# Fused attention and two feed-forward layers on one core: rounding queries and keys of all units on ScalarE

## The chip, the cores and the metric

The kernel runs on one core of a Trainium2 chip. The metric is the device time of one execution in microseconds, as the median over runs. A NeuronCore has TensorE (PE in the profile; its weight loads have a row of their own, PEld), VectorE (DVE), ScalarE (ACT), GpSimd (POOL) and SyncE (SP), which issues most DMAs. Each engine executes its own instructions in the order in which they were written to its queue.

## The reference

Three layers follow each other; the output of one is the input of the next.

```
scores = q k^T / sqrt(D), minus a bias from the cumulated max(s, 0); causal
attn   = softmax(scores);  x = attn v           # 4 batches x 8 heads, 576 positions, D = 64
h = x w_in;  x = (h * sigmoid(1.702 h)) w_out   # 2304 tokens, 512 -> 2048 -> 512
h = x w_in2; x = (s2 * max(h, 0)^2 + b2) w_out2
```

All tensors are fp32.

## The kernel before

TensorE multiplies in a rounded fp32 format (fp32r). To keep the precision, most operands are split in two: `hi` is the operand rounded to fp32r, `lo` the rest, and a product becomes a sum of two or three products. Rounding is a copy to an fp32r tile; the rest is a subtraction.

Attention is cut into eight **units**: for each of the 4 batches the first half of the query positions (320 rows, three chunks of 64, 128 and 128) and the second half (256 rows, two chunks of 128). A unit has 8 heads, so there are 64 head steps, numbered n = 0 to 63; the first-half units come first (n = 0 to 31), then the second-half ones (n = 32 to 63). While a unit's attention runs, TensorE works at the same time on the first feed-forward layer of the unit before it; `run` merges the two into one hand-made order for TensorE. The other engines' orders in this part are set by a scheduler that simulates the program's time line; in the first heads SP is written by hand too. After the last attention step come the rest of the first layer and the second layer, in an order written by hand for all engines.

One head goes through four places of the code:

- `prep` (L239 to L281) loads queries and keys of one head, in two copies on 128 partitions, as `raw`, and splits them. For n below 8 there is no split. From n = 8 on `hi` is `raw` rounded (L271, through `scaled`, L116 to L123, so it appears as L119 on ScalarE and L123 on VectorE); SP copies the queries' part of `hi` to `lo` (L272); VectorE subtracts for the queries' rest (L273) and GpSimd for the keys' (L274, `lo`). `hi` has 640 columns in the first half and 832 in the second. Each of `raw` and `hi` has two buffers, `lo` one. Of every second head it also rounds the values `v` (L279, L280).
- `qk` (L283 to L314) multiplies queries and keys chunk by chunk into PSUM (`ps`, two buffers); VectorE adds the mask and keeps the running extreme (L300; a chunk with 576 keys goes in two pieces of 288, so a second-half head has three pieces: 448, 288 and 288), ScalarE takes the exponential and its row sums (L306). After the last chunk VectorE makes the reciprocals of the sums (L310, L311), and the chunks of `x` are scaled by them: the last one on ScalarE (L119), the others on GpSimd (L121).
- `transposes` (L316 to L341) turns the probabilities of the head before by TensorE into `pst` (two buffers), in two groups in the first half and three in the second; ScalarE takes each group out rounded (`ph`, L338), VectorE the rest (L341).
- `pv` (L343 to L370) multiplies with the values, two heads back.

Beside these, `h_item` (L433 to L450) makes the hidden layer: `ph` by TensorE (L421), tanh on ScalarE (`th`, L442), a multiply on VectorE (L443), rounding on ScalarE (`g`, L447) and its rest on GpSimd (L448). `y_item` (L454 to L473) multiplies `g` with the second weights (L461).

The choice of the engine that rounds `hi` is one expression:

```
scaled(nc.scalar if n < 2 * H else nc.vector, hi[:, : u.n + J], raw[:, : u.n + J])
```

H is 8, so heads 8 to 15 are rounded on ScalarE and heads 16 to 63 on VectorE: 16 of them in the first half, 32 in the second.

Of the kernel before, what the change touches and what calls it, by code (L numbers as in the profile page):

```python
# [42 lines left out]
def f32(ap):  # L43
    return ap.bitcast(F32)
# [27 lines left out]
def fused_kernel(ctx: ExitStack, tc: tile.TileContext, qkT, vP, s, w1i, w1o, w2i, w2o, s2, b2, out):  # L72
    nc = tc.nc
    B, H, _, _ = qkT.shape
# [41 lines left out]
    def scaled(engine, out, in_, scale=1.0):  # L116

        if engine is nc.scalar:
            nc.scalar.activation(out, in_, AF.Copy, scale=scale)  # L119
        elif engine is nc.gpsimd:  # L120
            nc.gpsimd.tensor_scalar(out=out, in0=in_, scalar1=scale, scalar2=0.0, op0=ALU.mult, op1=ALU.add)  # L121
        else:
            nc.vector.tensor_scalar(out=out, in0=in_, scalar1=scale, scalar2=None, op0=ALU.mult)  # L123
# [50 lines left out]
    with ExitStack() as p1:  # L174
# [61 lines left out]
        def tile(shape, name, dtype=F32):  # L236
            return ap.tile([P, *shape], dtype, tag=name, name=name, bufs=size["bufs"][name])

        def prep(n):  # L239
            u, h = units[n // H], n % H  # L240
            J, nj = u.i1, len(u.keys)
            raw = tile([size["n"] + size["keys"]], "raw")

            r = u.b * H + h
            qc, kc = (slice(0, u.n), slice(u.n, u.n + J)) if u.half == 0 else (slice(J, J + u.n), slice(0, J))
            src = qkT[u.b, h, :, : u.n + J] if u.half == 0 else qkT[u.b, h, :, u.i0 :]
            heads[n] = t = {"x": {}, "qc": qc, "kc": kc}

            def beside(to):
                nc.sync.dma_start(to[D:R, kc], rows_d[0, r, :, :J])  # L250
                nc.sync.dma_start(to[D:R, qc], rows_d[1, r, :, u.i0 : u.i1])

            if n < H:
                nc.sync.dma_start(raw[:D, : u.n + J], src[:D])
                if n > 0:
                    beside(raw)
            else:
                nc.sync.dma_start(raw[:, : u.n + J], src)
            if h % 2 == 0:
                vraw = tile([size["blocks"], P], "vraw")  # L260
                nc.sync.dma_start(vraw[:, :nj, :], vP[u.b, h // 2, :, :nj, :])
                vs[n] = vs[n + 1] = vraw
            if n < H:
                t["parts"] = [(raw, R)]
                return


            hi = tile([size["n"] + size["keys"]], "hi", F32R)
            lo = tile([size["n"] + size["keys"]], "lo", F32R)
            beside(f32(lo))  # L270
            scaled(nc.scalar if n < 2 * H else nc.vector, hi[:, : u.n + J], raw[:, : u.n + J])  # L271
            nc.sync.dma_start(f32(lo[:D, qc]), f32(hi[:D, qc]))  # L272
            nc.vector.tensor_tensor(hi[D:, qc], raw[D:, qc], f32(hi[D:, qc]), ALU.subtract)  # L273
            nc.gpsimd.tensor_tensor(lo[:D, kc], raw[:D, kc], f32(hi[:D, kc]), ALU.subtract)  # L274
            t["parts"] = [(lo, R), (hi, P)]
            if h % 2 == 0:
                v = tile([size["blocks"], 4, D], "v", F32R)
                src = vraw[:, :nj].rearrange("p j (a d) -> p j a d", a=2)
                scaled(nc.gpsimd if n < 2 * H else nc.vector, v[:, :nj, 0:4:3, :], src)  # L279
                nc.gpsimd.tensor_tensor(v[:, :nj, 1:3, :], src, f32(v[:, :nj, 0:4:3, :]), ALU.subtract)  # L280
                vs[n] = vs[n + 1] = v  # L281
# [106 lines left out]
        def prep_to(n):  # L388
            while n_prep[0] <= min(n, limit - 1):
                prep(n_prep[0])  # L390
                n_prep[0] += 1
# [633 lines left out]
```

## Time and profile before

| | |
|---|---|
| median of 3 runs | 1046.09 us (1045.94 to 1046.18) |
| the profiled execution | 1047.54 us |
| its span, first to last instruction | 1045.7 us |
| mean granted clock of TensorE | 0.997 |
| busy: TensorE, its weight loads | 1006.4 us (96%), 926.0 us (89%) |
| busy: VectorE, ScalarE, GpSimd | 655.7 us (63%), 589.7 us (56%), 347.1 us (33%) |

The table gives the busy time of each engine over the whole span, which is an average over parts with different limits. "PE busy" counts matmuls that overlap each other. The attention steps of the first-half units run up to about 300 us, those of the second-half units from there to about 595 us; what follows has no attention.

### The profile page before, as it was taken

To read this page: it belongs to the slowest core of one execution; us is meant where nothing else is said; L and a number is where in the kernel's file an instruction comes from. 1 tells how busy PE (TensorE), PEld (TensorE's weight loads), DVE (VectorE), ACT (ScalarE), POOL (GpSimd) and SP (SyncE) were. 2 spreads that over 40 slices of the span, in tenths; PEclk is the share of its full clock that TensorE was granted. 3 is DMA by queue.
4 is the path that set the end of the run, shared out by engine and by line. 5 is a ranking of instruction groups with operands and counts; after the bars stand their busy time and mean duration, and the time that the engine had idled before them with its cause. 6 is when DMAs were issued, how large, how long until landed. Compare 5 with 4: busy or idle time off the path is not lost.

```text
span 1045.7 us, 17713 instructions
## 1 busy us (share of the span) xinstructions
PE 1006.4 (96%) x6312; PEld 926.0 (89%) x6312; DVE 655.7 (63%) x1426; ACT 589.7 (56%) x1316; POOL 347.1 (33%) x381
## 2 busy tenths in 40 slices
PE   5889999999999999999999999999999999999998
PEld 3458999999989999999999999999989989899897
DVE  4689877566558788788878556566575333632232
ACT  4889856556626656656656645566464343543342
POOL 1115535335325346345435322011033442311110
PEclk9998999999999999999999999999999999999999
DMA  5675422122032232232221067766126436352321
GB/s 177 192 246 190 125 85 78 47 84 57 9 122 68 76 91 76 76 95 72 84 92 56 21 247 225 257 217 228 51 91 234 149 132 229 123 201 96 126 71 61
DMA packets 52879, 129.58 MB, mean 124 GB/s; under 512 B 7068, under 2 KB 19480, under 8 KB 52792
## 3 DMA queue, kind: packets, MB, share of 16 engines
q1 hardware_dynamic: 52584, 128.32, 37.3%
q8 instruction: 50, 0.82, 0.3%
q14 instruction: 37, 0.30, 0.1%
q10 hardware_dynamic: 208, 0.13, 0.0%
HBM read 95.45 MB, written 28.90 MB: 119 GB/s over the span
## 4 chain that ended last, share of the span: by engine, by line
PE 77%; DVE 12%; ACT 5%; DMA 3%; issue 2%; SPq 1%; POOL 0%; ACTq 0%; DVEq 0%; POOLq 0%
PE py L756 18%; PE py L461 15%; PE ph L421 14%; PE sum_p L730 6%; PE ph L806 5%; PE ps L294 4%; PE pst L332 4%; DVE hi L123 3%; PE sum_r L730 3%; PE po L359 3%; PE py L697 2%; DMA pair<-w1i 2%; DVE x L300 2%; PE sum_q L730 2%; ACT x L306 1%
## 5 line engine op out<-in xcount | busy, mean ns | idle before, releaser
L421 PE MATMUL ph<-xT,wi 128*128 128x320 f32 (+1 forms) x1536 | 244.9, 304 | 6.3 <-DVE th L443 2.6
L756 PE MATMUL py<-wo,g 128*128 128x512 f32 x864 | 223.1, 394 | 0.6 <-DVE g L793 0.6
L421 PEld LDWEIGHTS ph<-xT,wi 128*128 128x128 f32 x1536 | 215.6, 191 | 8.5 <-DVE th L443 3.2
L461 PE MATMUL py<-g,wo 128*128 128x320 f32 (+1 forms) x1344 | 215.3, 304 | 0.0
L461 PEld LDWEIGHTS py<-g,wo 128*128 128x128 f32 x1344 | 188.0, 189 | 0.9
L756 PEld LDWEIGHTS py<-wo,g 128*128 128x128 f32 x864 | 160.6, 188 | 26.2 <-DVE g L793 0.9
L448 POOL TENSOR_TENSOR g<-th,g 128x320 fp32r<-128x320 f32 (+1 forms) x128 | 113.0, 885 | 133.5 <-ACT g L447 124.2
L306 ACT ACTIVATE x<-x,m 64x64 f32<-64x64 f32 (+2 forms) x160 | 89.4, 559 | 99.7 <-DVE m L300 98.1
L274 POOL TENSOR_TENSOR lo<-raw,hi 64x576 fp32r<-64x576 f32 (+1 forms) x56 | 67.8, 1211 | 122.7 <-issue 57.1
L300 DVE CUSTOM_DVE_ANT_0 x<-ps,mask 64x64 f32<-64x64 f32 (+2 forms) x160 | 68.0, 426 | 51.6 <-PE ps L294 49.7
L332 PE MATMUL pst<-ident,x 128*128 128x128 f32 (+2 forms) x480 | 86.2, 288 | 10.0 <-DVE ph L341 8.2
L793 POOL TENSOR_TENSOR g<-odd,g 128x768 fp32r<-128x768 f32 x16 | 30.5, 1904 | 183.3 <-ACT g L790 183.3
L121 POOL TENSOR_SCALAR x<-x,tot 64x64 f32<-64x64 f32 (+1 forms) x96 | 49.5, 523 | 93.5 <-DVE tot L311 47.6
L730 PE MATMUL sum_p<-xs,part 128*128 128x384 f32 x384 | 78.5, 339 | 1.4 <-ACT e L828 1.2
L338 ACT ACTIVATE ph<-pst 64x256 fp32r<-64x256 f32 (+2 forms) x144 | 67.1, 473 | 20.7 <-PE pst L332 19.3
L332 PEld LDWEIGHTS pst<-ident,x 128*128 128x128 f32 (+2 forms) x480 | 54.8, 136 | 25.1 <-DVE ph L341 13.2
L730 PEld LDWEIGHTS sum_p<-xs,part 128*128 128x128 f32 x384 | 69.2, 188 | 7.4 <-ACT e L828 1.7
L442 ACT ACTIVATE th<-ph 128x320 f32<-128x320 f32 (+1 forms) x128 | 51.6, 403 | 42.2 <-PE ph L421 40.4
L443 DVE SCALAR_TENSOR_TENSOR th<-th,ph 128x320 f32<-128x320 f32 (+1 forms) x128 | 57.5, 449 | 27.5 <-ACT th L442 26.5
L447 ACT ACTIVATE g<-th 128x320 fp32r<-128x320 f32 (+1 forms) x128 | 56.4, 440 | 32.2 <-DVE th L443 31.7
L806 PE MATMUL ph<-xs,wi 128*128 128x384 f32 x384 | 71.8, 335 | 0.0
L828 ACT ACTIVATE e<-sum_p 128x384 f32<-128x384 f32 x48 | 23.5, 489 | 84.9 <-PE sum_p L730 84.9
(108 smaller groups left out, 1666.3 us busy)
## 6 DMA issues: line engine op xcount, KB each, us to landing
part<-parts_d SPq DMA_DIRECT2D x32, 512.0 KB
raw<-qkT SPq DMA_DIRECT2D x32, 416.0 KB
pair<-w1o SPq DMA_DIRECT2D x16, 512.0 KB
pair<-w1i SPq DMA_DIRECT2D x16, 512.0 KB
pair<-w2i SPq DMA_DIRECT2D x16, 512.0 KB
pair<-w2o SPq DMA_DIRECT2D x16, 512.0 KB
parts_d<-part SPq DMA_DIRECT2D x16, 512.0 KB
raw<-qkT SPq DMA_DIRECT2D x24, 320.0 KB
```

Source lines behind the costliest of these rows:

```text
L274: nc.gpsimd.tensor_tensor(lo[:D, kc], raw[:D, kc], f32(hi[:D, kc]), ALU.subtract)
L300: nc.vector.tensor_tensor_reduce(out=x[:w, j0:j1], in0=ps[:w, : j1 - j0], in1=mask[:w, WIDE - a0 + j0 : WIDE - a0 + j1], scale=-1.0 / ROOT ...
L306: nc.scalar.activation(x[:w, :a1], x[:w, :a1], AF.Exp, bias=least, scale=-1.0, accum_out=tot[:w, c : c + 1])
L332: nc.tensor.transpose(ps[: j1 - j0, at : at + a1 - a0], t["x"][c][: a1 - a0, j0:j1], ident[: a1 - a0, : a1 - a0])
L338: nc.scalar.activation(t["ph"][:rows, base:end], ps[:rows, :m], AF.Copy)
L421: nc.tensor.matmul(ph[:, :n], wi[f][:, a, cc * P : (cc + 1) * P], x[cc][:, b, :n], start=(k == 0), stop=(k == 3 * NC - 1),)
L443: nc.vector.scalar_tensor_tensor(out=th[:, :n], in0=th[:, :n], scalar=1.0, in1=ph[:, :n], op0=ALU.add, op1=ALU.mult)
L448: nc.gpsimd.tensor_tensor(g[:, 1, :n], th[:, :n], f32(g[:, 0, :n]), ALU.subtract)
L461: nc.tensor.matmul(py[:, :n], wo[f][:, a, wc], g_t[ui, f][:, b, :n], start=(k == 0), stop=(k == 3 * G - 1))
L730: nc.tensor.matmul(ps[:, :N2], w[:, a, c0 : c0 + P], x[kind, k // 3][:, b, :], start=(first and k == 0), stop=(k == 5), skip_group_check=n ...
L756: nc.tensor.matmul(y_sums[t], g2[f % 2][:, a, t * P : (t + 1) * P], wo2[f][:, b, :], start=(first and k == 0), stop=end)
L806: nc.tensor.matmul(ps[:, :N2], wi2[f][:, a, cc * P : (cc + 1) * P], x[f"{cc // 2 + 1}{n + 1}", cc % 2][:, b, :], start=(k == 0), stop=(k = ...
```

## The change

The rounding of `hi` is done on ScalarE for every head from 8 on; heads 16 to 63 had it on VectorE. Nothing else in the text of the kernel changes.

```
--- before.py
+++ after.py
@@ -268,7 +268,7 @@
             hi = tile([size["n"] + size["keys"]], "hi", F32R)
             lo = tile([size["n"] + size["keys"]], "lo", F32R)
             beside(f32(lo))
-            scaled(nc.scalar if n < 2 * H else nc.vector, hi[:, : u.n + J], raw[:, : u.n + J])
+            scaled(nc.scalar, hi[:, : u.n + J], raw[:, : u.n + J])
             nc.sync.dma_start(f32(lo[:D, qc]), f32(hi[:D, qc]))
             nc.vector.tensor_tensor(hi[D:, qc], raw[D:, qc], f32(hi[D:, qc]), ALU.subtract)
             nc.gpsimd.tensor_tensor(lo[:D, kc], raw[:D, kc], f32(hi[:D, kc]), ALU.subtract)
```

The scheduler makes new orders from it. Those of TensorE and SP are the same as before; those of ScalarE, VectorE and GpSimd differ from head 16 on.

VectorE in the step of head 48, before (x is the head's probabilities, ps its scores; 448 and 288 are the widths of the pieces):

```order
L300 ISA x,m<-ps,mask 128x448
L300 ISA m 128x1
L408 TENSOR_TENSOR xT<-xraw,xT 128x256 x2
L443 SCALAR_TENSOR_TENSOR th<-th,ph_5815 128x256
L300 ISA x,m<-ps,mask 128x288
L300 ISA m 128x1
L123 TENSOR_SCALAR hi<-raw 128x832
L300 ISA x,m<-ps,mask,m 128x288
L300 ISA m 128x1
L273 TENSOR_TENSOR hi<-raw,hi 64x256
L310 TENSOR_SCALAR tot_71<-tot_71 128x2
L311 RECIPROCAL tot_71<-tot_71 128x2
```

The same piece now:

```order
L300 ISA x,m<-ps,mask 128x448
L300 ISA m 128x1
L408 TENSOR_TENSOR xT<-xraw,xT 128x256
L443 SCALAR_TENSOR_TENSOR th<-th,ph_5815 128x256
L300 ISA x,m<-ps,mask 128x288
L300 ISA m 128x1
L300 ISA x,m<-ps,mask,m 128x288
L300 ISA m 128x1
L273 TENSOR_TENSOR hi<-raw,hi 64x256
L310 TENSOR_SCALAR tot_71<-tot_71 128x2
L311 RECIPROCAL tot_71<-tot_71 128x2
```

The rounding stood between the second and the third piece; now the two pieces follow each other.

ScalarE in the same step, before (the exponentials L306, the rounding g of the hidden layer, the take-out of `po` L369, the scaling of x, and the take-outs of the three transposed groups L338):

```order
L306 ACTIVATE x,tot_71<-x,m 128x448
L447 ACTIVATE g<-th 128x256
L306 ACTIVATE x,tot_71<-x,m 128x576
L369 ACTIVATE xraw<-po 64x256
L119 ACTIVATE x<-x,tot_71 128x576
L338 ACTIVATE ph<-pst 64x256
L338 ACTIVATE ph<-pst 128x512
L338 ACTIVATE ph<-pst 128x384
```

The same step now:

```order
L306 ACTIVATE x,tot_71<-x,m 128x448
L447 ACTIVATE g<-th 128x256
L119 ACTIVATE hi<-raw 128x832
L306 ACTIVATE x,tot_71<-x,m 128x576
L369 ACTIVATE xraw<-po 64x256
L119 ACTIVATE x<-x,tot_71 128x576
L338 ACTIVATE ph<-pst 64x256
L338 ACTIVATE ph<-pst 128x512
L338 ACTIVATE ph<-pst 128x384
```

The rounding has been put ahead of the second exponential; the rest of the step is in the same order.

ScalarE in the step of head 49, as a difference:

```order
 L306 ACTIVATE x,tot_72<-x,m 128x448
+L119 ACTIVATE hi<-raw 128x832
 L306 ACTIVATE x,tot_72<-x,m 128x576
-L369 ACTIVATE xraw<-po 64x256
-L338 ACTIVATE ph<-pst 64x256
 L119 ACTIVATE x<-x,tot_72 128x576
+L369 ACTIVATE xraw<-po 64x256
+L338 ACTIVATE ph<-pst 64x256
 L407 ACTIVATE xT<-xraw 128x256
 L338 ACTIVATE ph<-pst 128x512
```

Here the scaling of x, which needs the reciprocal of this head's sums, has also moved: it stood behind the take-out of the first transposed group and now stands ahead of it.

## Rows read from the trace of the kernel before

**Rows 1.** The page: its first line, and busy time of each engine, share, instructions.

```profile
span 1045.7 us, 17713 instructions
...
PE 1006.4 (96%) x6312; PEld 926.0 (89%) x6312; DVE 655.7 (63%) x1426; ACT 589.7 (56%) x1316; POOL 347.1 (33%) x381
```

**Rows 2.** Busy time by stretch: PE, PEld, DVE, ACT, POOL, PEclk, DMA share, GB/s.

```profile
125.00:160.00 35.00, 33.81 (x238) 31.89 (x238) 25.34 (x72) 21.41 (x61) 16.24 (x25) 1.00 0.32 94
160.00:300.00 140.00, 140.00 (x993) 136.30 (x992) 85.53 (x234) 80.04 (x222) 56.75 (x80) 1.00 0.18 51
300.00:395.00 95.00, 88.89 (x620) 85.19 (x620) 74.86 (x169) 53.23 (x125) 44.92 (x42) 1.00 0.31 95
395.00:595.00 200.00, 194.73 (x1589) 191.10 (x1588) 157.78 (x379) 126.41 (x314) 98.13 (x101) 1.00 0.24 73
```

**Rows 3.** Waits of the weight loads, 300 to 595 us: total us, times, longest.

```profile
PEld pst L332 <- DVE ph L341: 13.2, 19, 1.4
PEld ps L294 <- POOL lo L274: 1.7, 1, 1.7
PEld ps L294 <- DVE m L300: 1.7, 3, 1.1
```

**Rows 4.** Timeline of VectorE, step of head 48: start us, duration us, instruction, idle before.

```profile
451.25 1.95 DVE L123 TENSOR_SCALAR hi<-raw 128x832 fp32r<-128x832 f32 x1
453.12 0.50 DVE L300 CUSTOM_DVE_ANT_0 x<-ps,mask,m 128x288 f32<-128x288 f32 x1
...
456.25 0.42 DVE L341 TENSOR_TENSOR ph<-pst,ph 64x256 fp32r<-64x256 f32 x1 [0.67 <-ACT ph L338]
```

**Rows 5.** Timeline of ScalarE, start of the second half and step of head 48.

```profile
305.98 0.44 ACT L442 ACTIVATE th<-ph 128x320 f32<-128x320 f32 x1 [6.61 <-PE ph L421]
...
450.99 0.42 ACT L447 ACTIVATE g<-th 128x256 fp32r<-128x256 f32 x1 [0.24 <-DVE th L443]
453.67 0.78 ACT L306 ACTIVATE x<-x,m 128x576 f32<-128x576 f32 x1 [2.26 <-DVE m L300]
...
455.04 0.78 ACT L119 ACTIVATE x<-x,tot 128x576 f32<-128x576 f32 x1
455.84 0.86 ACT L338 ACTIVATE ph<-pst 64x256 fp32r<-64x256 f32 x2
```

**Rows 6.** Timeline of the weight loads, third groups of heads 47's and 48's steps.

```profile
446.74 0.31 PEld L332 LDWEIGHTS pst<-ident,x 128*128 128x128 f32 x3 [0.74 <-DVE ph L341]
...
456.72 0.31 PEld L332 LDWEIGHTS pst<-ident,x 128*128 128x128 f32 x3 [1.05 <-DVE ph L341]
```

**Rows 7.** Waits of ScalarE, 300 to 595 us.

```profile
ACT x L306 <- DVE m L300: 71.1, 49, 2.7
```

**Rows 8.** Groups by line and shape, whole span: busy us, mean ns, idle before.

```profile
L123 DVE TENSOR_SCALAR hi<-raw 128x832 fp32r<-128x832 f32 x32 | 53.6, 1677 | 2.5 <-DMA raw<-qkT 2.3 <-issue 0.2
...
L442 ACT ACTIVATE th<-ph 128x256 f32<-128x256 f32 x64 | 24.2, 377 | 25.7 <-PE ph L421 24.9
...
L123 DVE TENSOR_SCALAR hi<-raw 128x640 fp32r<-128x640 f32 x16 | 15.4, 961 | 0.0
...
L790 ACT ACTIVATE g<-odd 128x768 fp32r<-128x768 f32 x16 | 13.6, 848 | 0.5
...
L119 ACT ACTIVATE hi<-raw 128x640 fp32r<-128x640 f32 x8 | 5.8, 727 | 0.0
```

**Rows 9.** Timeline of VectorE, start of the second half.

```profile
301.35 0.59 DVE L123 TENSOR_SCALAR hi<-raw 128x832 fp32r<-128x832 f32 x1 [1.45 <-DMA raw<-qkT]
...
304.35 1.28 DVE L123 TENSOR_SCALAR hi<-raw 128x832 fp32r<-128x832 f32 x1 [0.70 <-DMA raw<-qkT]
```

**Rows 10.** Timeline of GpSimd, start of the second half and step of head 48.

```profile
302.25 1.43 POOL L274 TENSOR_TENSOR lo<-raw,hi 64x576 fp32r<-64x576 f32 x1 [13.16 <-DMA x_d<-y]
...
450.64 1.42 POOL L274 TENSOR_TENSOR lo<-raw,hi 64x576 fp32r<-64x576 f32 x1 [1.10 <-PE ps L294]
452.02 0.72 POOL L448 TENSOR_TENSOR g<-th,g 128x256 fp32r<-128x256 f32 x1
```

More of the change, by code (lines that the diff above doesn't have):

```diff
@@ L270, in prep @@
             beside(f32(lo))
-            scaled(nc.scalar if n < 2 * H else nc.vector, hi[:, : u.n + J], raw[:, : u.n + J])
+            scaled(nc.scalar, hi[:, : u.n + J], raw[:, : u.n + J])
             nc.sync.dma_start(f32(lo[:D, qc]), f32(hi[:D, qc]))
```

## The prediction

> **What bounds the kernel.** I read the busy shares first, then the busy time by stretch, then the waits of TensorE's weight loads, then the timeline of one attention step. TensorE is busy for 1006.4 of 1045.7 us [rows 1], so a change on VectorE and ScalarE can pay only where TensorE waits for them. The stretches tell where that is. From 160 to 300 us, where most of the first-half heads concerned run, TensorE is busy for the whole 140 us, and in the 35 us before for 33.81; from 300 to 595 us, where the second-half heads run, it is busy for 88.89 of 95 and 194.73 of 200 us, while VectorE stands at 74.86 and 157.78 us, about 79% [rows 2]. So the stretch that can move is the second one, and VectorE is its most loaded helper.
>
> Matmuls overlap, so a gap in "PE busy" is smaller than what the gap costs. I take the idle time ahead of the weight loads instead: 13.2 us in 19 waits, the longest 1.4 us, all of the same kind. They are the transposes of the probabilities (L332), held up by VectorE's low part of the transposed probabilities (L341); beside them stand 1.7 us of waits of the score product for the masked maximum (L300) [rows 3].
>
> Why L341 is late is seen in one step, that of head 48. Each step transposes in three groups and psT has two buffers, so group three needs group one taken out by L338 and L341. In the step the score product has three pieces, each taken by one L300. At 451.25 us the second is done, and VectorE starts the rounding `hi`, for a head two further on, which takes 1.95 us; only at 453.12 us comes the third piece [rows 4]. The exponential of 576 columns on ScalarE cannot start before 453.67 us; the total, its reciprocal, the scaling (L119 of `x`, 455.04 us) and the take-out of group one (L338, 455.84 us) follow in its queue [rows 5]. L341 runs at 456.25 us [rows 4], and the weights of group three load at 456.72 us after 1.05 us of waiting [rows 6]. The whole chain hangs on `hi`. ScalarE's waits agree: its exponential waited 71.1 us in 49 waits for the maximum of L300 [rows 7].
>
> Why does `hi` take so long? 32 of them average 1677 ns [rows 8]. The first, with GpSimd idle, took 0.59 us [rows 9, 10]. Head 48's step has GpSimd at work on `lo` from 450.64 and on `g` until 452.74 us [rows 10]; `hi` ended at 453.20 us, 0.46 us after GpSimd was free. The end of the score product releases both `lo` of the next head and `hi` of the one after it, so they collide in step after step.
>
> **The change, part by part.**
>
> *VectorE, second half.* It loses 32 roundings of 1.677 us, 53.6 us [rows 8]. Its share in the stretch falls from 79% to about 61%, and L300's third piece can start as soon as the second ends.
>
> *ScalarE, second half.* It gains 32 roundings of 832 columns, a shape that the trace lacks on ScalarE. The same operation took 727 ns for 640 columns and 848 ns for 768 [rows 8]; that is 0.945 ns a column, so 0.91 us here (an estimate from those rows), 29 us in all. ScalarE goes from (53.23 + 126.41) of 295 us, 61%, to 71%. Bounds for one: not under the 0.85 us of 768 columns, not over 727 x 832 / 640 ns = 0.95 us; I take 0.91, from the slope, since the 768-column row is near.
>
> *What that does to a step.* In head 48's step ScalarE's new queue is exponential, `g`, `hi`, exponential of 576. `g` ran at 450.99 for 0.42 us [rows 5], so `hi` would run from 451.41 to 452.32, when the third piece has long been taken. The exponential starts at 452.32 instead of 453.67 us, 1.35 us earlier. From there to the weight load the chain is the same length, 456.72 - 453.67 = 3.05 us, so group three could load at 455.37; TensorE wants it at 456.72 - 1.05 = 455.67. The stall of 1.05 us is gone with 0.3 us to spare.
>
> In other steps a `th` (377 ns [rows 8]) stands there too, and another `th` ahead of the first exponential: each takes 0.38 us off, so the relief lies between 1.35 and about 0.6 us. With 1.35 us everywhere nearly all of the 13.2 us goes, since the longest wait is 1.4; with 0.6 everywhere 13.2 - 19 x 0.6 = 1.8 us stay at least, and some 3 us as the waits are uneven. One more thing keeps some of it: in eleven second-half steps (counted in the two orders) the new order puts the scaling of `x` ahead of the take-out of group one, where it stood behind it. In most of these TensorE did not wait at all before. In the step before head 48's it did, for 0.74 us [rows 6], and so it does eight heads later; there I expect half to stay, 0.7 us. With 1 us for the thinner relief, a third of the 3 us above, 1.7 us are left over: **11.5 us gained**.
>
> *The waits of 1.7 us on L300.* There are three [rows 3]. What stands ahead of that L300 is not always `hi`, so they may go or stay: I book nothing, and 1.7 us for the range.
>
> *The start of the second half.* The first `hi` is on the path (TensorE waits there for `lo` of its first head, 1.7 us [rows 3]). It took 0.59 us on VectorE [rows 9] and 0.91 us on ScalarE, so **0.3 us lost**. The second `hi` waits for its load, until 304.35 us [rows 9], and now holds up ScalarE, with a `th` behind it; that one ran at 305.98 us, when its product was there [rows 5]. 304.35 + 0.91 = 305.26 us comes before it, so I book nothing.
>
> *First half, 16 roundings.* VectorE loses 961 ns each, ScalarE gains 727 [rows 8]. No TensorE idle time is there to win between 160 and 300 us [rows 2]. None should arise: the first half transposes in two groups, for which two buffers are enough, so L341 has a whole step of slack. ScalarE's share goes from 57%, 80.04 of 140 us, to 65% at most (16 x 0.727 = 11.6 us more). Nothing, both ways. In the 35 us before, TensorE lacks 1.2 us [rows 2], which I leave as they are.
>
> *Queues.* SP's order is the same, and TensorE's too; `lo` on GpSimd and the copy of `hi` to `lo` on SP wait for `hi` as before, and the head concerned is scored a step later or more; a step takes some 10 us, as from 446.74 to 456.72 us [rows 6]. The subtraction L273 behind `hi` on VectorE now waits for ScalarE: in head 48's step until 452.32, with nothing behind it but the total, which needs the exponential anyway.
>
> **Sum.** -11.5 + 0.3 = -11.2 us. Against the profiled execution, 1047.5 us outside and 1045.7 us in span, that is 1036.3 us. That execution stands 1.45 us above the median of the runs shown, so the prediction in terms of the median, 1046.1 us, is **1034.9 us**.
>
> **The rivals.**
>
> *Half goes.* The wait moves from VectorE to ScalarE. For it: L341 itself waited mostly for L338 on ScalarE, as in head 48's step (0.67 us ahead of 456.25) [rows 4], and ScalarE runs in order. Against it: ScalarE was late there because it waited for L300. If the 0.6 us of relief is halved by the operations in front, 19 x 0.3 = 5.7 us are gained: 1040 us, between 1037 and 1043.
>
> *Nothing moves.* The exponential starts when it did, because `hi`, `g` and `th` fill the time that VectorE's `hi` filled (0.91 + 0.41 + 0.38 = 1.70 us against 1.68). Then the time stays at 1046 us. It needs all three ahead of the exponential in every step that stalls, and the order of the change has that in seven of the 19.
>
> *Slower.* Beside that, the scaling of `x`, now ahead of the take-out of group one in eleven steps, delays it by its 0.78 us [rows 5] in each: 8.6 us, 1054.7 us. It decides where ScalarE reaches the scaling less than about 1.6 us before TensorE wants group three (0.78 for the scaling, about 0.4 for the take-out, 0.42 for L341 [rows 4, 5]). A row speaks for the cause, the slower engine: an undisturbed VectorE needs 0.59 us, ScalarE 0.91. Against it: VectorE was undisturbed once in 32. The Trainium skill has a rule that would have this case: "ScalarE: Activation LUTs", Rules for kernel authors, gives multiplications to VectorE, as up to about 3 times faster per element in 16 bits. By that rule the step would lose rather than gain; the one undisturbed row agrees, the mean of the 32 rows does not.
>
> **How the numbers follow.** A measurement of this kernel can tell about 0.2%, 2 us, from no change. The forecast has 0.73, half 0.13, nothing 0.07, slower 0.07. Faster by over 0.2% is the first two, 0.86. The range reaches down to all waits gone, the 1.7 us on L300 included (13.2 + 1.7 = 14.9 us, 1031.2), and up to most of the half case, 1042.5; nothing and slower, 0.14, stay outside, with the edges.
>
> **What would show it.** In the profile of the changed kernel: the 832-column roundings on ScalarE at 0.88 to 0.95 us; no row of VectorE for them; VectorE at 60 to 64% and ScalarE at 70 to 74% of the second-half stretch, which is about 11 us shorter; TensorE's weight loads waiting 1 to 3 us for L341 in place of 13.2; from 160 to 300 us no TensorE idle time. It is wrong if the weight loads keep over 6 us of waits there, whatever their releaser is called, or if new ones stand under ScalarE's name in the first half.

## The result and the profile after

The change takes **1035.2 us** (median of 5 runs, 1034.44 to 1037.59), the kernel before 1046.09 us beside it (median of 5, 1045.73 to 1048.11): a ratio of 0.9899, 95% interval 0.9881 to 0.9917. The profiled execution took 1034.67 us, 1032.8 in span, at a mean granted clock of 0.997, as before.

The page's busy time, which answers to [rows 1]:

```profile
span 1032.8 us, 17760 instructions
PE 1003.0 (97%) x6312; PEld 926.7 (90%) x6312; DVE 608.9 (59%) x1378; ACT 626.6 (61%) x1364; POOL 346.3 (34%) x381
```

VectorE and ScalarE have changed places. By stretch, with the columns of [rows 2], the last one cut where attention now ends:

```profile
125.00:160.00 35.00, 34.19 (x244) 32.82 (x243) 22.25 (x72) 24.14 (x67) 15.59 (x24) 1.00 0.31 90
160.00:300.00 140.00, 140.00 (x993) 136.30 (x992) 73.95 (x218) 87.05 (x230) 56.44 (x80) 1.00 0.19 57
300.00:395.00 95.00, 92.47 (x661) 89.93 (x659) 66.32 (x170) 66.67 (x149) 47.80 (x46) 1.00 0.31 94
395.00:584.00 189.00, 187.72 (x1548) 186.11 (x1548) 133.18 (x347) 139.45 (x322) 94.34 (x98) 1.00 0.24 73
```

From 300 to 584 us TensorE is busy for 280.19 of 284 us, where it had 283.62 of 295. VectorE stands at 199.50 us there, 70%, and ScalarE at 206.12, 73%.

What TensorE's weight loads wait for from 300 to 584 us, which answers to [rows 3]:

```profile
PEld pst L332 <- DVE ph L341: 2.5, 4, 0.8
PEld ps L294 <- DVE hi L273: 1.2, 1, 1.2
PEld ps L294 <- POOL lo L274: 1.2, 1, 1.2
PEld py L461 <- POOL g L448: 0.6, 2, 0.3
PEld ps L294 <- DVE m L300: 0.3, 1, 0.3
PEld ps L294 <- POOL g L448: 0.3, 1, 0.3
```

The wait for L341 fell from 13.2 us in 19 waits to 2.5 in 4; the second line is new. All waits together are 6.1 us, where they were 16.6.

Where the span became shorter is read at three starts: the first score product of head 32 (304.64 us before, 301.90 after), the first matmul of the second layer (615.27, 602.37), and the end. Between the first two the time fell from 310.63 to 300.47 us, by **10.16 us** (called "the second half" below); after them it is 430.5 us in both. Of the 2.74 us ahead of head 32, 1.40 are there by the first score product of head 14, ahead of the first rounding that was moved. So 12.9 us between two profiled executions is more than the change's share; the medians differ by 10.9.

The groups of the rounding and of the subtraction behind it, beside [rows 8]:

```profile
L119 ACT ACTIVATE hi<-raw 128x832 fp32r<-128x832 f32 x32 | 28.7, 898 | 6.5 <-DMA raw<-qkT 3.5 <-POOL lo L274 1.5 <-issue 0.6
L273 DVE TENSOR_TENSOR hi<-raw,hi 64x256 fp32r<-64x256 f32 x32 | 25.0, 781 | 4.2 <-ACT hi L119 2.7
L119 ACT ACTIVATE hi<-raw 128x640 fp32r<-128x640 f32 x24 | 17.6, 734 | 0.7 <-PE ps L294 0.3
```

The first row is the price that the prediction estimated. The second is one that it did not price. Before, the same 32 subtractions took 434 ns each:

```profile
L273 DVE TENSOR_TENSOR hi<-raw,hi 64x256 fp32r<-64x256 f32 x32 | 13.9, 434 | 1.0
```

Head 48's step now begins at 439.69 us instead of 448.08. ScalarE in it, from the timeline, beside [rows 5]:

```profile
441.92 0.42 ACT L447 ACTIVATE g<-th 128x256 fp32r<-128x256 f32 x1
442.29 0.90 ACT L119 ACTIVATE hi<-raw 128x832 fp32r<-128x832 f32 x1
443.19 0.78 ACT L306 ACTIVATE x<-x,m 128x576 f32<-128x576 f32 x1
...
444.89 0.78 ACT L119 ACTIVATE x<-x,tot 128x576 f32<-128x576 f32 x1 [0.25 <-DVE tot L311]
445.86 0.38 ACT L338 ACTIVATE ph<-pst 64x256 fp32r<-64x256 f32 x1 [0.19 <-PE pst L332]
```

The exponential starts 443.19 - 439.69 = 3.50 us into the step, against 453.67 - 448.08 = 5.59 before. The take-out of group one no longer runs late: it waits 0.19 us for TensorE itself. Over the second half ScalarE's exponentials wait a third of what they did in [rows 7]:

```profile
ACT x L306 <- DVE m L300: 21.7, 22, 1.8
```

### The profile page after: what moved, and what is told of

The parts are those of the page before. It is cut to its first block, busy times and chain, and to the rows that moved or that the text cites. A ratio compares the mean times of both kernels' runs of the same rounds, so it can differ in the third digit from the quotient of the medians.

```text
span 1032.8 us, 17760 instructions
## 1 busy us (share of the span) xinstructions
PE 1003.0 (97%) x6312; PEld 926.7 (90%) x6312; DVE 608.9 (59%) x1378; ACT 626.6 (61%) x1364; POOL 346.3 (34%) x381
## 4 chain that ended last, share of the span: by engine, by line
PE 86%; DVE 6%; ACT 2%; DMA 2%; issue 1%; POOL 1%; SPq 0%; DVEq 0%; ACTq 0%; POOLq 0%
PE py L756 18%; PE ph L421 17%; PE py L461 17%; PE sum_p L730 6%; PE ps L294 6%; PE ph L806 5%; PE pst L332 5%; PE po L359 4%; PE sum_r L730 3%; PE py L697 2%; PE sum_q L730 2%; PE po L353 1%; DVE hi L273 1%; DVE wo L165 1%; DVE pair L156 1%
## 5 line engine op out<-in xcount | busy, mean ns | idle before, releaser
L306 ACT ACTIVATE x<-x,m 64x64 f32<-64x64 f32 (+2 forms) x160 | 89.3, 558 | 47.7 <-DVE m L300 46.7
L300 DVE CUSTOM_DVE_ANT_0 x<-ps,mask 64x64 f32<-64x64 f32 (+2 forms) x160 | 68.2, 426 | 57.5 <-PE ps L294 55.9
L338 ACT ACTIVATE ph<-pst 64x256 fp32r<-64x256 f32 (+2 forms) x144 | 68.3, 476 | 35.5 <-PE pst L332 33.9
L341 DVE TENSOR_TENSOR pl<-pst,ph 128x512 fp32r<-128x512 f32 (+1 forms) x88 | 53.2, 605 | 38.1 <-ACT ph L338 37.6
L121 POOL TENSOR_SCALAR x<-x,tot 64x64 f32<-64x64 f32 (+1 forms) x96 | 48.8, 516 | 75.9 <-DVE tot L311 53.6
```

The costliest lines, as they stand in the source:

```text
L300: nc.vector.tensor_tensor_reduce(out=x[:w, j0:j1], in0=ps[:w, : j1 - j0], in1=mask[:w, WIDE - a0 + j0 : WIDE - a0 + j1], scale=-1.0 / ROOT ...
L306: nc.scalar.activation(x[:w, :a1], x[:w, :a1], AF.Exp, bias=least, scale=-1.0, accum_out=tot[:w, c : c + 1])
L338: nc.scalar.activation(t["ph"][:rows, base:end], ps[:rows, :m], AF.Copy)
```

## The experiments

Each ratio is to runs of the kernel before on the same chip; runs of one table block shared a chip.

| run | edit | median us (range, n) | ratio, 95% | second half, us |
|---|---|---|---|---|
| the change | | 1035.2 (1034.44 to 1037.59, 5) | 0.9899, 0.9881 to 0.9917 | 300.47 |
| | | | | |
| e1 | second half alone | 1036.57 (1034.52 to 1038.93, 6) | 0.9921, 0.9905 to 0.9938 | 300.42 |
| e2 | first half alone | 1046.23 (1044.9 to 1047.77, 12) | 1.0007, 0.9994 to 1.0019 | 310.84 |
| e3 | before, `lo` on VectorE | 1035.81 (1034.09 to 1036.91, 6) | 0.9911, 0.9894 to 0.9927 | 300.45 |
| e4 | change, rounding twice | 1045.22 (1043.75 to 1049.86, 12) | 1.0003, 0.9991 to 1.0015 | 308.08 |
| | | | | |
| e8 | before, scaling on GpSimd | 1038.86 (1037.7 to 1041.05, 6) | 0.9932, 0.9915 to 0.9949 | 304.16 |
| e7 | change, L273 on GpSimd | 1032.76 (1031.93 to 1035.46, 4) | 0.988, 0.9857 to 0.9902 | 298.17 |
| e9 | change, `lo` on VectorE | 1038.71 (1038.11 to 1041.06, 5) | 0.9931, 0.9914 to 0.9949 | 302.46 |
| e6 | change, head 32 as before | 1034.86 (1034.34 to 1035.73, 4) | 0.9892, 0.9874 to 0.991 | 298.17 |
| | | | | |
| again | the change once more | 1036.56 (1033.58 to 1037.83, 6) | 0.99, 0.9882 to 0.9918 | 300.76 |
| e10 | e6 and e7 together | 1031.82 (1029.99 to 1034.84, 5) | 0.986, 0.9843 to 0.9877 | 298.10 |
| e11 | e10, `v` on ScalarE too | 1036.84 (1036.29 to 1038.34, 5) | 0.991, 0.9897 to 0.9923 | 301.15 |

### Which half pays: e1 and e2

```
# e1, L271
scaled(nc.vector if 2 * H <= n < 4 * H else nc.scalar, ...)
# e2, L271
scaled(nc.scalar if n < 4 * H else nc.vector, ...)
```

> Only the second-half heads (32 to 63) are rounded on ScalarE; heads 16 to 31 stay on VectorE as before. Theory (all of the gain comes from the second-half steps): within 1.5 us of the change, 1034 to 1037 us, waits for L341 at 2.5 us as with the change. Rival (part of the gain is made in the first half, since from head 16 to head 32 the two traces differ by 1.3 us): 1036.5 us or more, and head 32's first score product comes 1 us or more later after head 16's than with the change.

> Only heads 16 to 31 are moved to ScalarE; the second half stays on VectorE as before. Theory: no change, 1045 to 1047 us, 13 us of waits for L341. Rival (the first half gains 1.3 us): 1044 to 1045 us.

The 32 roundings of the second half bring all of it: in e1 the second half lasts 300.42 us, with 2.2 us of waits for L341. In e2 it lasts 310.84 us, with 13.5 us in 19 waits, as before, and the total cannot be told from no change. One sign of e1's rival did show: from head 16's first score product to head 32's it is 160.86 us in e1 and 159.79 in the change, 1.07 apart. But a second execution of the change (the run `again`, below) has 160.68 there, e2 160.39 and the kernel before 160.75, so single executions differ by as much. e1's median, 1036.57 us, lies in both ranges; e2, with no gain from the first half, decides against the rival. TensorE had nothing to win in the first half, and ScalarE there took 16 more roundings without holding it up.

### Is it the collision that makes `hi` long: e3

```
# e3: L271 as before; L274
(nc.gpsimd if n < 4 * H else nc.vector).tensor_tensor(lo[:D, kc], ...)
```

> The kernel before, with the keys' subtraction (lo, L274) of the second half moved from GpSimd to VectorE, so that GpSimd is not at work when VectorE rounds hi. VectorE then does 0.75 us more in each step, just ahead of hi. Theory (hi is long because it waits for GpSimd): hi falls from 1.68 to about 0.5 to 0.7 us, the sum of both is about 1.25 us, 0.4 us less than before in the chain, and the time falls by 3 to 7 us, to 1039 to 1043. Rival (hi takes 1.6 us by its size and type): hi stays near 1.6, VectorE has 0.75 us more in the chain of every step, and the time rises by 8 us or more, to 1054.

In the groups of e3 the rounding is still on VectorE, but GpSimd's `lo` is gone from beside it:

```profile
L123 DVE TENSOR_SCALAR hi<-raw 128x832 fp32r<-128x832 f32 x32 | 28.2, 880 | 1.7 <-DMA raw<-qkT 1.7
L274 DVE TENSOR_TENSOR lo<-raw,hi 64x576 fp32r<-64x576 f32 x32 | 23.9, 746 | 0.1
```

1677 ns became 880, which is more than the 0.5 to 0.7 us expected, because it is the mean of two kinds. In 16 steps `hi` took 0.58 to 0.60 us, as in head 49's:

```profile
452.59 0.58 DVE L123 TENSOR_SCALAR hi<-raw 128x832 fp32r<-128x832 f32 x1
```

In the other 16 it took 1.1 to 1.7 us, each time beside a rest of `g` or `v` on GpSimd. So the collision is what made it long. But `hi` and `lo` together take VectorE 1.63 us a step, about what `hi` alone took, and yet the gain is as large as the change's, against the 3 to 7 us expected. The working of the prediction has no place for that; head 48's step of e3, which begins at 440.87 us, shows how it comes about. VectorE:

```profile
443.51 0.45 DVE L300 CUSTOM_DVE_ANT_0 x<-ps,mask 128x288 f32<-128x288 f32 x1
...
443.88 0.74 DVE L274 TENSOR_TENSOR lo<-raw,hi 64x576 fp32r<-64x576 f32 x1
444.55 1.12 DVE L123 TENSOR_SCALAR hi<-raw 128x832 fp32r<-128x832 f32 x1
445.60 0.50 DVE L300 CUSTOM_DVE_ANT_0 x<-ps,mask,m 128x288 f32<-128x288 f32 x1
```

ScalarE:

```profile
446.14 0.78 ACT L306 ACTIVATE x<-x,m 128x576 f32<-128x576 f32 x1 [0.33 <-DVE m L300]
446.82 0.19 ACT L306 ACTIVATION_READ_ACCUMULATOR x<-x,m 128x1 f32 x1
447.04 1.12 ACT L338 ACTIVATE ph<-pst 64x256 fp32r<-64x256 f32 x2
448.06 0.77 ACT L119 ACTIVATE x<-x,tot 128x576 f32<-128x576 f32 x1
```

The third piece starts 445.60 - 443.88 = 1.72 us after the end of the second, against 1.87 us in [rows 4], and the exponential 5.27 us into the step, against 5.59 before: nearly as late. But ScalarE now takes out two groups (L338, x2) ahead of the scaling, where before the scaling stood ahead of the take-out [rows 5], so the take-out begins 6.17 us into the step instead of 7.76. A late third piece need not stall TensorE: here it stalled it through what stood behind it in ScalarE's queue. The order that the scheduler wrote for e3, with `lo` in VectorE's queue as well, bears most of the delay. What is left in e3 is

```profile
PEld pst L332 <- DVE ph L341: 4.8, 11, 1.1
```

of 13.2 us. That is more than the change leaves; the second half is as short because the steps of heads 32 and 33 last 14.97 us in e3 and 15.89 in the change.

### How much goes through the scaling: e8

```
# e8: L271 as before; L313
engine = nc.scalar if k == last and n < 4 * H else nc.gpsimd
```

> The kernel before, hi on VectorE, but in the second half the scaling of the last chunk of x is done by GpSimd instead of ScalarE, so that the take-out of transposed group one (L338) no longer stands behind an instruction that needs this head's row sums. hi stays as long as it was. Theory A (the stall comes from ScalarE's order, made for a short hi: the late third piece hurts only through the scaling ahead of the take-out): hi stays at 1.6 us or more and yet the waits for L341 fall from 13.2 to under 6 us, the time to 1036 to 1041 us. Theory B (the late third piece holds up the take-out through the exponential as well, which stands ahead of it too): the waits stay over 9 us, the time is 1043 us or more.

Here `hi` stays on VectorE, and long (1625 ns); only the scaling leaves ScalarE's queue. The waits of the weight loads:

```profile
PEld pst L332 <- DVE ph L341: 6.9, 15, 1.3
PEld ps L294 <- POOL lo L274: 1.7, 1, 1.7
PEld py L461 <- POOL g L448: 0.9, 2, 0.5
```

13.2 us became 6.9: about half of the stall went through the scaling ahead of the take-out, and the other half is there without it. The waits lie between the two expectations, and so the cause is shared; the time, 7.4 us under the kernel before, lies in theory A's range. The scheduler wrote new orders for e8 in other places too, so the share of one half is an estimate from these waits and not a clean measure.

### How much room ScalarE has: e4

```
# e4: the change, and below L271
if n >= 4 * H:
    scaled(nc.scalar, hi[:, : u.n + J], raw[:, : u.n + J])
```

> The changed kernel with the rounding of second-half heads issued twice on ScalarE (the same values written again): 0.9 us more of ScalarE in each of 32 steps. Theory (the margin left in a step is some 0.3 us, ScalarE is now in the chain): the stalls come back, 8 to 14 us more than the change, 1043 to 1049 us, and the waits of the weight loads for L341 are over 8 us. Rival (ScalarE has idle time enough in each step, the chain had hung on VectorE alone): 1035 to 1038 us.

The weight loads' waits in the second half (the line numbers are two higher):

```profile
PEld pst L334 <- DVE ph L343: 9.3, 9, 2.4
PEld ps L296 <- POOL lo L276: 3.5, 1, 3.5
```

0.9 us more on ScalarE per step puts stalls back under the same name, though in other steps (2.4 us in head 39's, 1.5 in those of heads 43, 51 and 59). The median is that of the kernel before; in the traced execution the second half gives back 7.6 of its 10.16 us. `hi` also comes 0.9 us later for those that read it, but apart from the 3.5 us for `lo` at the start the waits stand at the transposes and not at the score product. So what ScalarE took over fits, with less than 0.9 us to spare.

### The subtraction that grew: e7 and e9

L273 took 434 ns before and 781 after. In head 50's step, one of the four that still stall, the timeline shows why that matters. GpSimd:

```profile
460.59 1.44 POOL L274 TENSOR_TENSOR lo<-raw,hi 64x576 fp32r<-64x576 f32 x1 [4.77 <-ACT x L306]
461.99 0.73 POOL L448 TENSOR_TENSOR g<-th,g 128x256 fp32r<-128x256 f32 x1
```

ScalarE and VectorE:

```profile
460.59 0.90 ACT L119 ACTIVATE hi<-raw 128x832 fp32r<-128x832 f32 x1
461.55 1.46 DVE L273 TENSOR_TENSOR hi<-raw,hi 64x256 fp32r<-64x256 f32 x1
463.04 0.42 DVE L443 SCALAR_TENSOR_TENSOR th<-th,ph 128x256 f32<-128x256 f32 x1
463.38 0.16 DVE L310 TENSOR_SCALAR tot<-tot 128x2 f32<-128x2 f32 x1
```

Weight loads:

```profile
465.89 0.31 PEld L332 LDWEIGHTS pst<-ident,x 128*128 128x128 f32 x3 [0.54 <-DVE ph L341]
```

The collision has found another instruction. `hi` and `lo` (of different heads) still start together, at 460.59 us; on ScalarE `hi` is done in 0.90 us while `lo` takes 1.44. So L273, which waits for `hi`, begins beside `lo`, goes on beside `g` and ends at 463.01 us, 0.29 after GpSimd is free, as `hi` used to end after GpSimd. `th` and the total come behind it. The Trainium skill, "SBUF — State Buffer", Who interferes with whom, states that a VectorE instruction with two SBUF inputs contends with a GpSimd instruction that reads SBUF. The rows agree: 1.46 us here, and 0.42 in head 48's step of the kernel before, where GpSimd was idle:

```profile
453.67 0.42 DVE L273 TENSOR_TENSOR hi<-raw,hi 64x256 fp32r<-64x256 f32 x1
```

```
# e7: the change; L273
(nc.vector if n < 4 * H else nc.gpsimd).tensor_tensor(hi[D:, qc], ...)
# e9: the change; L274
(nc.gpsimd if n < 4 * H else nc.vector).tensor_tensor(lo[:D, kc], ...)
```

> The changed kernel with the queries' subtraction (L273) of second-half heads moved from VectorE to GpSimd, where it stands behind lo and cannot meet it. In the changed kernel L273 takes 0.78 us instead of 0.43, 1.46 in head 50's step, and stands ahead of the row sums. Theory (the 2.5 us left of waits for L341 come from L273's meeting with lo): these waits fall under 1.2 us, the time by 1 to 3 us against the change, 1032 to 1034.5 us. Rival (they come from ScalarE's queue): waits of 2 us or more, 1034.5 to 1037 us.

> The changed kernel with lo (L274) of the second half on VectorE too: hi on ScalarE, both subtractions on VectorE, so nothing of prep meets GpSimd. VectorE's chain between the second and third score piece gets 0.75 us of lo, in place of the 1.68 us of hi before. Theory: L273 back at 0.43 us, the waits for L341 between 1 and 3 us, within 1.5 us of the change, 1033 to 1036.5 us. Rival (any 0.75 us in VectorE's chain costs as hi did): 1038 us or more.

Both separate the two subtractions. In e7, where VectorE is rid of L273, the weight loads wait as follows:

```profile
PEld ps L294 <- POOL lo L274: 1.9, 1, 1.9
PEld pst L332 <- DVE ph L341: 1.8, 5, 0.8
PEld ps L294 <- DVE m L300: 0.7, 1, 0.7
```

The stalls in the steps of heads 42, 50 and 58, 0.54 to 0.55 us each, shrank to 0.17. The waits for L341 did not fall under the expected 1.2 us: 0.80 us stay in head 39's step, where they were 0.84, and 0.47 are new in head 33's. The second half is 2.3 us shorter than the change's and the median 2.4 us under it; but the two intervals overlap, so that this step is a gain rests on the rows. In e9 VectorE has both subtractions, and the weight loads wait longer:

```profile
PEld pst L332 <- DVE ph L341: 3.1, 7, 0.8
PEld ps L294 <- issue: 2.4, 1, 2.4
PEld ps L294 <- DVE m L300: 1.7, 3, 0.7
```

The second half is 2.0 us longer than the change's; the medians, from different chips, are 3.5 us apart, with intervals that overlap by a little. The theory missed: L273 was not back at 0.43 us but took 605 ns on the mean. The meeting with `lo` is gone, but in 12 of the 32 steps L273 now meets `g` on GpSimd and takes 0.81 to 1.08 us. `lo`, 802 ns, stands in VectorE's chain, and in the steps of heads 48 and 56 TensorE waits 0.74 us for L300: that costs more than the collision did.

### The first head of the second half: e6

```
# e6: the change; L271
scaled(nc.vector if n == 4 * H else nc.scalar, ...)
```

> The changed kernel with the very first second-half head (32) rounded on VectorE, where it met no GpSimd work before. Theory (0.3 us of the start of the second half is the slower rounding, and L273 is late there for its meeting with lo): the first steps of the second half are 0.3 to 1.3 us shorter, the time 0 to 1.5 us less than the change, 1033 to 1036 us. Rival (the loads set the start): no difference that shows.

At the start of the second half the change had on VectorE:

```profile
300.68 2.50 DVE L273 TENSOR_TENSOR hi<-raw,hi 64x256 fp32r<-64x256 f32 x1
```

and e6, with head 32's rounding back on VectorE:

```profile
300.32 0.59 DVE L123 TENSOR_SCALAR hi<-raw 128x832 fp32r<-128x832 f32 x1 [1.41 <-DMA raw<-qkT]
300.95 0.42 DVE L273 TENSOR_TENSOR hi<-raw,hi 64x256 fp32r<-64x256 f32 x1
```

The 2.50 us are a subtraction that met `lo` and the rest of `v` on GpSimd; they are the 1.2 us of weight-load wait for L273. The steps of heads 32 and 33 last 14.09 us in e6, 15.89 in the change (16.23 in its second execution) and 16.04 before. So 1.8 us are to be had there, more than expected. The medians, from different chips, show 0.3 us of them, which is no difference that these runs can tell.

### A version faster than both: e10, and one step too far: e11

e10 has the edits of e6 and e7; e11 adds, at L279, `nc.scalar` for `v` in the second half.

> The changed kernel once more, on the chip of the next two, so that they can be set beside it. All theories: 1034 to 1037 us, a ratio of 0.988 to 0.992 to the kernel before; from head 32's first score product to the first matmul of L697, 300 to 301 us.

> The changed kernel with both small amendments: head 32 rounded on VectorE, and L273 of the second half on GpSimd. Theory (the two gains lie at different places, one in the first two steps of the second half, the other in the steps where L273 met lo): 296 to 298 us from head 32's first score product to L697, and 2 to 4 us less than the change on the same chip, 1031 to 1033 us. Rival (they are the same gain, made at the start): 298 us or more, no better than either alone.

> As the kernel with both amendments, and the rounding of the values v (0.82 us in every second step of the second half) taken from VectorE to ScalarE too. Theory (VectorE no longer sets the end of any step but two or three, and ScalarE is now the busier): no gain, 0 to 2 us more than with both amendments. Rival (every us off VectorE still pays): 1 to 3 us less.

e10 is the fastest kernel of the study: 1031.82 us against 1036.56 for the change on the same chip, with intervals that do not overlap (0.9843 to 0.9877, 0.9882 to 0.9918); from e7 it cannot be told apart. Its second half, 298.10 us, is no shorter than with e6 or e7 alone, so the rival's figure (298 us or more) came true: the two gains do not add up. The steps of heads 32 and 33 take 15.14 us in e10, near e7's 15.26 and not e6's 14.09, and from head 34 on e10 and e7 are alike, 282.96 and 282.90 us against the change's 284.59. The gains do lie at different places, but e7's edit takes most of e6's away. In e11 the weight loads show what became late:

```profile
PEld pst L332 <- DVE ph L341: 3.5, 11, 0.6
PEld py L461 <- POOL g L448: 2.0, 2, 1.0
PEld ps L294 <- POOL lo L274: 1.8, 1, 1.8
```

Eleven waits for L341 in place of five. From 300 to 584 us ScalarE is busy for 214.25 us and VectorE for 168.40: VectorE has become the engine with room, and the next thing moved onto ScalarE costs, as e4 had shown from the other side. It costs 5.0 us in the median and 3.05 in the second half, where 0 to 2 had been expected.

## Why the prediction was right, point by point

**What bounds it: right.** The gain came out of the weight loads' waits for L341, 13.2 to 2.5 us, and almost all of it in the second half. 310.63 to 300.47 us is 10.16; the waits account for 10.0: -10.7 for L341 and -1.4 for L300, +1.2 for L273 and +0.9 for `g`. The wait for `lo` (1.7 us before, 1.2 after) lies ahead of head 32's first score product.

**The figure: closer than its working.** 1034.9 us was forecast and 1035.2 measured, but that is in part luck. The working wanted 11.2 us in the second half, and the traces show 10.16: too much was booked for L341 (11.5 for 10.7), nothing for L300 (1.4 gained), for L273 (1.2 lost) and for `g` (0.9 lost). And the second execution of the change, on another chip, is 9.8 us under the kernel before in the median, where this pair has 10.9.

**The sign of being wrong: at its edge.** The forecast was to be wrong if the weight loads kept over 6 us of waits in the stretch, whatever the releaser. They keep 6.1 us, 5.5 in the second execution. What holds it up is that 1.2 of the 6.1 us are the wait for `lo`, which was there before, and that only 2.5 are for L341.

**The price on ScalarE: right.** 898 ns, estimated 0.91 us, inside the bounds from the 640 and 768 columns. VectorE lost the 53.6 us of roundings that were booked.

**Head 48's step: right, and too careful.** `hi` runs right behind `g`, and the exponential right behind `hi`, as foreseen. The exponential starts 2.1 us earlier in the step where 1.35 was worked out: the working let the second piece and `g` stand where they were, and they came earlier too.

**Left-over stalls: the size right (2.5 us, predicted 1.7), the steps wrong.** Half of the waits in the steps of heads 47 and 55 was to stay, because the scaling stands ahead of the take-out there. Both are gone, since the scaling itself now comes in time. What is left is in the steps of heads 39, 42, 50 and 58; the last three shrink when L273 leaves VectorE (e7), and the cause of the first stays open.

**Start of the second half: not seen.** 0.3 us were to be lost for a slower first rounding. The first two steps last 15.89 us and 16.23 in the two executions of the change, and 16.04 before and 15.87 in e2, where they are as before: no difference that can be told. What the change does lose in them is L273's 2.50 us, which e6 takes back.

**First half at nothing: right** (e2, and 140.00 of 140 us in the second stretch above).

**The waits on L300, booked at nothing:** 1.7 us became 0.3.

**The step that failed is "Queues".** It put nothing but the total behind L273 and let L273 itself keep its 434 ns. But `hi` on ScalarE is done while GpSimd still works on the `lo` that started with it, so the collision passed from `hi` to L273: 32 x (781 - 434) ns = 11.1 us more work on VectorE. The prediction's own rows held this: it let L273 start at 452.32 us, and in [rows 10] GpSimd is at work until 452.74. The 11.1 us are over half of the 20.5 by which VectorE's 199.50 us exceed the 179.0 that were booked (232.64 - 53.6), and so most of why it stands at 70% of the stretch where 60 to 64 were predicted. It cost little where L273 still ends ahead of the exponential's sums, as in head 48's step (443.23 + 0.74 = 443.97 us, the exponential's sums at 443.87 + 0.19 = 444.06), although there L310, next in the queue, took 0.50 us beside `g` where it had taken 0.17; e7 shows what was left in it.

**What the chain left out.** The prediction followed the stall from `hi` to the weight load as if each link were fixed. e3 and e8 show that the order in ScalarE's queue is a link of its own, with 6.3 of the 13.2 us of waits in e8 and up to 8.4 in e3: the kernel before stalls because `hi` is long *and* because ScalarE scales ahead of the take-out. That the scheduler wrote this order because it counts `hi` short on VectorE fits both runs; it was argued, not shown by one that feeds it the longer time.

**The rivals.** "Half goes" and "nothing moves" needed ScalarE to be late; its exponentials wait a third of what they did, and 2.5 us of stalls are left. "Slower" fell on its price. Its cause was a slower engine. Beside GpSimd's `lo` VectorE took 1677 ns, ScalarE 898. The Trainium skill, "ScalarE: Activation LUTs", Rules for kernel authors, would leave the rounding, a multiplication, to VectorE. Where GpSimd leaves VectorE alone the rows agree, 0.58 us in half of e3's steps against 0.90 on ScalarE; on the mean they do not, 880 ns in e3 and 1677 before.

## What to carry to other kernels

Price an instruction where it stands, with its neighbours, and not by its best row: here a rounding cost 0.59 us alone and 1.68 us in the steady state. When one is moved off a contended place, ask which instruction now runs beside the neighbour that stays, for the collision may pass to it. And where an in-order queue was planned with durations that the chip does not keep, two repairs are worth a trial, taking the long instruction out and another order: here the first brought 10.9 us, and the second 7.4 (e8) to 9.6 (e3, where both came together).

## What the runs showed of the hardware that was not expected

A subtraction of 64 x 256 on VectorE took 0.42 us undisturbed and up to 2.50 us beside two GpSimd instructions in a row; it ended 0.28 us after the second one. GpSimd's `lo` beside it took 1.41 to 1.44 us, as in [rows 10], so in these rows VectorE bore the wait. It is not always so: in head 48's step of e3 a rest of `g` on GpSimd took 1.10 us beside `lo` and `hi` on VectorE, against 0.73 in head 50's step above. ScalarE's rounding of 832 columns took 0.88 to 0.90 us in all 32 steps, beside GpSimd or not; VectorE's took 0.58 to 2.35. The same subtraction took 738 ns on GpSimd (e7): with the neighbour that it has, VectorE's mean of 781 ns was no better.
